# Expert weights split during the second mixture into the buffers that TensorE reads

## The chip, the cores and the metric

The kernel runs on one core of one Trainium2 chip. The metric is the device time of one execution in microseconds (us); lower is better. The kernel before took 1017.65 us, the median of three runs (1014.8 to 1020.23).

## What is computed

Three stages follow one another. Attention over 4 batches of 576 tokens gives x, 2304 tokens of width 512. A gated layer of width 1536 follows, then a mixture of 8 experts, of which each token takes the best two. In the reference, shortened:

```python
gate = 1 / (1 + exp(-(x @ w_gate)))          # first mixture: 2304 x 512 x 1536, twice
x = (gate * (x @ w_val)) @ w_out
noisy = x @ rg + log1p(exp(x @ rn)) * noise  # router, 8 experts
top2 = the two best experts of each token, weights = softmax of their two logits
for e in range(8):                           # second mixture
    h = relu(x[rows of e] @ w1[e])           # 512 x 1024
    out[rows of e] += weight * (h @ w2[e])   # 1024 x 512
```

## The kernel before, in words

Every fp32 operand of a large product is held as two fp16 halves, a high part and the rest, and a product is three fp16 matmuls (high by high, high by rest, rest by high). `split` (line 338) makes the halves of a tile: one activation on ScalarE writes the high part (line 339), one scalar_tensor_tensor on VectorE the rest (line 340). Ahead of a split stands a scale: the sum of squares of the whole matrix (two quarters by ScalarE, line 604, two by VectorE, line 602), added over the partitions by a small matmul with ones on TensorE and turned into a power of two by three short VectorE instructions (`norm2`, line 70).

The first mixture works through nine chunks of 256 tokens. `stage1` (line 373) makes gate times value of a chunk, `stage2` (line 402) multiplies by the output matrix, `tokens` (line 413) writes the 128 rows of a tile to DRAM as halves (`xs<-row`, line 429), turns them by a transposing DMA (`xt<-row`, line 432) and multiplies them by the router matrix (`pl`, line 439); `route` (line 492) picks the experts and scatters (token, weight) into a table in DRAM (line 554). The output matrix lies in the tiles `wob[0..5]`.

Beside the chunks runs `presplits` (line 577). For each of 16 units, the matrices w1 and w2 of 8 experts, it loads four quarters of 512 KB (`f<-w`, line 591; nine buffers), squares, scales and splits them into a tile `hl` (two buffers) and stores the halves to DRAM (`wsp<-hl`, line 619). One step is taken after each piece of a chunk; what is left ahead of the last chunk is taken in one go (`drain(pre)`, line 919).

The second mixture, `moe2` (line 719), goes expert by expert. `first2` (line 673) makes the hidden layer, eight tiles of 24 matmuls each, whose results ScalarE reads out (lines 684 and 685) and VectorE finishes (line 686, the low half of `hT`). `second2` (line 688) makes five tiles of 24 matmuls, which ScalarE scales (line 699) and GpSimd adds into the output by an indirect DMA (line 700). The rows of the next expert are fetched meanwhile: `fetch` (line 649) reads its part of the table on SP's queue, `gather` (line 663) collects rows by an indirect DMA of GpSimd, `turn` (line 670) turns them by a transposing DMA on SP's queue. w1 and w2 have two buffers each; `wload2` (line 645) loads the halves of expert e+2, 2 MB at a time, once expert e has left a buffer.

The instructions of each engine stand in an order that a scheduler makes from the program's order and from its own estimate of when each is ready; SP's queue too starts its DMAs in the order in which they stand, and one that waits holds up those behind it.

Of the kernel before, what the change touches and what calls it, by code (L numbers as in the profile page):

```python
# [9 lines left out]
F32 = mybir.dt.float32  # L10
# [30 lines left out]
SNAP = 6  # L41

# [14 lines left out]
class Kern:  # L57
# [284 lines left out]
    @staticmethod  # L342
    def flat(t):
        n = len(t.shape) - 1
        names = "abcd"[:n]
        return t if n == 1 else t.rearrange(f"p {' '.join(names)} -> p ({' '.join(names)})")
# [121 lines left out]
    def dram_open(self):  # L468
        dp = self.ctx.enter_context(self.tc.tile_pool(name="dram", bufs=1, space=DRAM))
        self.xs = dp.tile([N + PADS, 2 * DM], F16, name="xs")  # L470
        self.meta = dp.tile([P * NBLK, 2], I32, name="meta")
        self.wsp = dp.tile([E, P, 16384], F16, name="wsp")
# [99 lines left out]
    def presplit_open(self):  # L572
        self.ps_ctx = ExitStack()
        self.pp = self.ps_ctx.enter_context(self.tc.tile_pool(name="psp", bufs=2, side="right"))
        self.iv2 = self.cp.tile([P, 2, E], F32, name="iv2")

    def presplits(self):

        nc, a, pp = self.nc, self.a, self.pp
        units = [(e, j) for e in range(E) for j in range(2)]  # L580
# [44 lines left out]
    def inverse_scales(self):  # L625

        self.iw = self.cp.tile([P, E], F32, name="iw")
        self.nc.vector.scalar_tensor_tensor(self.iw, self.iv2[:, 0, :], 2.0 ** 19, self.iv2[:, 1, :], op0=ALU.mult, op1=ALU.mult)
# [89 lines left out]

    def moe2(self):

        mt, xe, xg = self.mt, self.xe, {}
        for e in range(E):
# [10 lines left out]
            if e + 2 < E:  # L733
                self.wload2(e + 2, 0)
# [10 lines left out]
            if e + 2 < E:  # L745
                self.wload2(e + 2, 1)

    def overflow(self):
# [23 lines left out]
        mt = cp.tile([P, 2], I32, name="mto")  # L772
        trips = nc.values_load(cnt[0:1, 0:1], min_val=0, max_val=E * EB)
        with self.tc.For_i(0, trips, 1):
# [18 lines left out]
            flat = lambda t: t.rearrange("p a b c -> p (a b c)")  # L793
            for j, w in enumerate((self.w1[0], self.w2[0])):
                nc.sync.dma_start(flat(w), self.wsp[ds(e, 1), :, j * 8192 : (j + 1) * 8192].rearrange("a p f -> p (a f)"))
# [7 lines left out]
    def build(self):  # L803
# [112 lines left out]
        for c in range(2, NCH):  # L916
            nxt = second_part(c - 1)
            if c == NCH - 1:
                drain(pre)
                self.ps_ctx.close()  # L920
                self.early_open()
                self.wload2(0, 0)
                self.inverse_scales()
                self.xe_tile(0)
# [65 lines left out]
```

## Time and profile before

| what | value |
|---|---|
| median of three runs | 1017.65 us |
| profiled execution, its own time | 1019.11 us |
| its span, first to last instruction | 1017.4 us |
| mean granted TensorE clock, share of full | 0.972 |
| TensorE matmuls busy | 962.5 us (95%) |
| VectorE busy | 469.4 us (46%) |
| ScalarE busy | 467.1 us (46%) |
| GpSimd busy | 214.3 us (21%) |
| DMA moved | 185.60 MB, mean 182 GB/s |

The attention fills about the first 185 us, the chunks of the first mixture 185 to 600 us, the second mixture the rest. A share over the whole span hides that the stages differ: VectorE and ScalarE do most of their work in the first 600 us. TensorE is the busiest engine by far, and the chain that ended last is a chain of TensorE over the whole second mixture.

### The profile page before, as it was taken

The page shows a single profiled execution, that of the slowest core. Times are in us where ns is not written, and L with a number is a line of the kernel's source. Part 1 is how long each engine was busy: PE and PEld are TensorE (multiplying, and loading weights), DVE is VectorE, ACT ScalarE, POOL GpSimd, SP SyncE. Part 2 cuts the span into 40 slices and gives each one's busy share as a digit, 9 for nine tenths or more (in the row PEclk, how much of TensorE's full clock was granted, in tenths as well). Part 3 has the DMA queues.
Part 4 walks back from the last instruction along what each step waited for, and adds up shares of the span by engine and source line. Part 5 has one row for each costly group of instructions (what it writes and reads, how often), then busy time and mean ns, then how long its engine had stood idle before and what let it go on. Part 6 is the DMA issues. An engine that isn't in the chain of part 4 may idle for free. (4 is left out here: it accounts for less than half of the span.)

```text
span 1017.4 us, 18817 instructions
## 1 busy us (share of the span) xinstructions
PE 962.5 (95%) x7471; PEld 674.8 (66%) x7471; DVE 469.4 (46%) x1296; ACT 467.1 (46%) x971; POOL 214.3 (21%) x213
## 2 busy tenths in 40 slices
PE   6889899999999999899989988999999999999996
PEld 5666777778678877687767555656565666666663
DVE  2688998756666767575776250111111111111020
ACT  4667777645565656455654142332323232323231
POOL 1243455001010101010101124312212222222202
PEclk9898998999999999999989999999999999999998
DMA  8666675876657776657665848955758575755303
GB/s 258 216 216 237 218 214 193 332 208 183 192 188 218 233 227 212 205 165 216 187 208 202 264 136 149 224 186 126 195 124 197 123 197 123 197 123 115 41 11 41
DMA packets 137097, 185.60 MB, mean 182 GB/s; under 512 B 72752, under 2 KB 82096, under 8 KB 134960
## 3 DMA queue, kind: packets, MB, share of 16 engines
q1 hardware_dynamic: 127024, 163.64, 52.5%
q0 software_dynamic: 9984, 20.75, 11.3%
q8 instruction: 59, 0.97, 0.4%
q14 instruction: 30, 0.25, 0.1%
HBM read 113.13 MB, written 56.02 MB: 166 GB/s over the span
## 5 line engine op out<-in xcount | busy, mean ns | idle before, releaser
L389 PE MATMUL pg<-x,w 128*128 128x256 f16 (+3 forms) x3456 | 311.6, 251 | 1.6 <-DVE sg L396 0.9
L389 PEld LDWEIGHTS <-w 128*128 128x128 f16 x3456 | 273.8, 100 | 33.9 <-issue 2.6
L694 PEld LDWEIGHTS <-hT 128*128 128x128 f16 (+1 forms) x960 | 100.1, 104 | 105.9
L411 PE MATMUL px<-wo,gT 128*128 128x512 f16 x648 | 147.2, 379 | 0.0
L686 DVE TENSOR_TENSOR hT<-r,hT 128x312 f16<-128x312 f32 (+2 forms) x128 | 56.9, 481 | 149.7 <-ACT hT L685 149.7
L554 POOL DMA_INDIRECT meta<-mt,vi x36 | 37.9, 1054 | 353.5 <-DVE sg L396 196.7
L680 PE MATMUL ph<-xe,w1a 128*128 128x312 f16 (+2 forms) x768 | 104.6, 299 | 3.4 <-DMA xe<-xg 3.4
L699 ACT ACTIVATE y<-py,css 128x512 f32<-128x512 f32 (+1 forms) x40 | 27.5, 687 | 174.9 <-PE py L694 170.4
L411 PEld LDWEIGHTS <-gT 128*128 128x128 f16 x648 | 62.4, 98 | 66.6
L700 POOL DMA_INDIRECT out<-y,mts x40 | 62.5, 1562 | 200.4 <-ACT y L699 198.9
L694 PE MATMUL py<-w2a,hT 128*128 128x512 f16 (+1 forms) x480 | 104.4, 379 | 0.0
L694 PE MATMUL py<-w2b,hT 128*128 128x512 f16 (+1 forms) x480 | 104.3, 379 | 0.0
L680 PE MATMUL ph<-xe,w1b 128*128 128x312 f16 x768 | 102.4, 296 | 0.0
L684 ACT ACTIVATE r<-ph 128x312 f32<-128x312 f32 (+2 forms) x128 | 48.9, 428 | 114.2 <-PE ph L680 111.5
L340 DVE SCALAR_TENSOR_TENSOR hl<-f,scs,hl 128x1024 f16<-128x1024 f32 x64 | 81.4, 1283 | 40.3 <-ACT hl L339 39.9
L339 ACT ACTIVATE hl<-f,scs 128x1024 f16<-128x1024 f32 x64 | 72.8, 1144 | 56.7 <-DMA wsp<-hl 40.6
L680 PEld LDWEIGHTS <-w1a 128*128 128x128 f16 x768 | 75.7, 99 | 31.3 <-DMA xe<-xg 3.9
L680 PEld LDWEIGHTS <-w1b 128*128 128x128 f16 x768 | 75.1, 98 | 27.1
L697 DVE TENSOR_TENSOR css<-mts,iw 128x1 f32<-128x1 f32 (+1 forms) x40 | 6.3, 159 | 183.5 <-ACT y L699 178.1
L395 ACT ACTIVATE sg<-pg,gs 128x256 f32<-128x256 f32 (+3 forms) x144 | 55.4, 410 | 20.5 <-PE pg L389 20.2
L398 ACT ACTIVATE gT<-sg 128x256 f16<-128x256 f32 x108 | 44.1, 410 | 44.4 <-DVE sg L396 44.4
L665 POOL DMA_INDIRECT xg<-xs,mts x40 | 40.1, 1003 | 114.3 <-issue 45.8
(300 smaller groups left out, 948.4 us busy)
## 6 DMA issues: line engine op xcount, KB each, us to landing
f<-w SPq DMA_DIRECT2D x64, 512.0 KB, 5.8
wsp<-hl SPq DMA_DIRECT2D x64, 512.0 KB, 3.9
w1a<-wsp SPq DMA_DIRECT2D x4, 2048.0 KB, 7.7
w2a<-wsp SPq DMA_DIRECT2D x4, 2048.0 KB, 8.7
w1b<-wsp SPq DMA_DIRECT2D x4, 2048.0 KB, 8.0
w2b<-wsp SPq DMA_DIRECT2D x4, 2048.0 KB, 7.8
w<-wg SPq DMA_DIRECT2D x12, 512.0 KB, 5.7
w<-wv SPq DMA_DIRECT2D x12, 512.0 KB, 5.7
```

The lines of the kernel that those rows point to most:

```text
L339: self.nc.scalar.activation(hi, src, AF.Copy, scale=sc)
L340: self.nc.vector.scalar_tensor_tensor(lo, src, sc, hi, op0=ALU.mult, op1=ALU.subtract)
L389: nc.tensor.matmul(pg[:, j, s:e], w[:, l, k, fo : fo + P], self.xT[b][r][:, k, t0 : t0 + e - s], start=n == 0, stop=n == 3 * KT - 1)
L395: nc.scalar.activation(sg[:, s:e], pg[:, 0, s:e], AF.Tanh, scale=self.gate_scale(b, u))
L398: nc.scalar.activation(g[:, 0, :], sg, AF.Copy, scale=2.0 ** -16)
L411: nc.tensor.matmul(p, g[:, l, t * P : (t + 1) * P], self.wob[f // 2][:, r, f % 2, :], start=f + i == 0, stop=f == FT - 1 and i == 2)
L665: self.nc.gpsimd.indirect_dma_start(out=xg.rearrange("p a b -> p (a b)"), out_offset=None, in_=self.xs[:rows, :], in_offset=bass.IndirectO ...
L680: nc.tensor.matmul(p[:, : t1 - t0], w1[:, l, k, f * P : (f + 1) * P], xe[:, x, t0:t1], start=n == 0, stop=n == 3 * KT - 1)
L684: nc.scalar.activation(r, p[:, : t1 - t0], AF.Relu, scale=2.0 ** -19)
L686: nc.vector.tensor_sub(self.hT[:, 1, f, t0:t1], r, self.hT[:, 0, f, t0:t1])
L694: nc.tensor.matmul(py, self.hT[:, l, f, i * P : i * P + m], w2[:, w, f, :], start=n == 0, stop=n == 3 * F2T - 1)
L700: d = nc.gpsimd.indirect_dma_start(out=self.out, out_offset=bass.IndirectOffsetOnAxis(ap=mt[:m, 0:1], axis=0), in_=y[:m], in_offset=None, ...
```

## The change

Only experts 0 and 1 are split ahead and go through DRAM (`AHEAD2 = 2`). The weights of experts 2 to 7 are loaded as fp32 during the second mixture, quarter by quarter, into the seven tiles `wob`, which the first mixture has left. There they are squared and split, straight into the w1 or w2 buffer that TensorE will read; the squares themselves go into the high half of that buffer, as a place to throw them. A generator (`splits`) does nine steps for each of the 12 units; two steps are taken after the first layer of an expert and three after each tile of its second layer. A quarter's buffer is loaded again once its split is done. A loop for experts with too many rows (`overflow`), whose weights came from DRAM too, now splits them anew as well; that part of the diff is left out.

```diff
+AHEAD2 = 2
...
-        self.wsp = dp.tile([E, P, 16384], F16, name="wsp")
+        self.wsp = dp.tile([AHEAD2, P, 16384], F16, name="wsp")
...
-        units = [(e, j) for e in range(E) for j in range(2)]
+        units = [(e, j) for e in range(AHEAD2) for j in range(2)]
...
-    def inverse_scales(self):
-
-        self.iw = self.cp.tile([P, E], F32, name="iw")
-        self.nc.vector.scalar_tensor_tensor(self.iw, self.iv2[:, 0, :], 2.0 ** 19, self.iv2[:, 1, :], op0=ALU.mult, op1=ALU.mult)
+    def inverse_scale(self, e):
+
+        self.nc.vector.scalar_tensor_tensor(self.iw[:, e : e + 1], self.iv2[:, 0, e : e + 1], 2.0 ** 19, self.iv2[:, 1, e : e + 1], op0=ALU.mult, op1=ALU.mult)
...
+    def part_load(self, j, i, e):
+
+        t = self.flat(self.wob[self.nparts % len(self.wob)]).bitcast(F32)
+        self.nparts += 1
+        self.nc.sync.dma_start(t.rearrange("p (k f) -> p k f", k=(KT, F2T)[j] // 4), self.part_src(j, i, e))
+        return t
+
+    def halves(self, j, i, x):
+
+        k = (KT, F2T)[j] // 4
+        return [self.flat((self.w1, self.w2)[j][x][:, l, i * k : (i + 1) * k, :]) for l in range(2)]
+
+    def splits(self):
+
+        nc = self.nc
+        units = [(e, j) for e in range(AHEAD2, E) for j in range(2)]
+        quarters = [(j, i, e) for e, j in units for i in range(4)]
+        parts = []
+
+        def load(n):
+            while len(parts) < min(n, len(quarters)):
+                parts.append(self.part_load(*quarters[len(parts)]))
+        load(len(self.wob))
+        for n, (e, j) in enumerate(units):
+            while self.freed[j] < e - 1:
+                yield
+            sums = self.my.tile([P, 4], F32, tag="sq", name="sq")
+            for i in range(4):
+                t, junk = parts[4 * n + i], self.halves(j, i, e % 2)[0].bitcast(BF16)
+                if i % 2:
+                    nc.vector.scalar_tensor_tensor(junk, t, 1.0, t, op0=ALU.mult, op1=ALU.mult, accum_out=sums[:, i : i + 1])
+                else:
+                    nc.scalar.activation(junk, t, AF.Square, accum_out=sums[:, i : i + 1])
+                yield
+            m = self.my.tile([P, 1], F32, tag="sm1", name="sm1")
+            nc.vector.tensor_reduce(m, sums, axis=AX.X, op=ALU.add)
+            s, iv = yield from self.norm2(self.my, m, "sc2")
+            nc.vector.tensor_copy(self.iv2[:, j, e : e + 1], iv)
+            if j:
+                self.inverse_scale(e)
+            for i in range(4):
+                self.split(parts[4 * n + i], s, *self.halves(j, i, e % 2))
+                load(len(self.wob) + 4 * n + i + 1)
+                yield
...
+    def step2(self, n):
+        for _ in range(n):
+            next(self.splitter, None)
...
+        self.freed, self.nparts = [0, 0], 0
+        self.splitter = self.splits()
...
             for f in range(F2T):
                 self.first2(self.w1[e % 2], xe[e], f, spans)
-            if e + 2 < E:
-                self.wload2(e + 2, 0)
+            self.step2(2)
+            self.freed[0] = e + 1
...
-            if e + 2 < E:
-                self.wload2(e + 2, 1)
+                self.step2(3)
+            self.freed[1] = e + 1
...
-                self.inverse_scales()
+                for e in range(AHEAD2):
+                    self.inverse_scale(e)
```

In the built programs the order moves at these places.

**SP's queue in the first mixture**, around the rows of the tenth tile of 128 tokens (`hl` are halves to be stored, `f` the next quarters). Before:

```order
L591 DMA f<-w 128x2x512
L619 DMA wsp<-hl 128x2x1024
L591 DMA f<-w 128x2x512
L429 DMA xs<-row 128x1024
L432 DMA_TRANSPOSE xt<-row 128x8x128
L619 DMA wsp<-hl 128x2x1024
L591 DMA f<-w 128x2x512
L619 DMA wsp<-hl 128x2x1024
```

After:

```order
L431 DMA xs<-row 128x1024
L434 DMA_TRANSPOSE xt<-row 128x8x128
L431 DMA xs<-row 128x1024
L434 DMA_TRANSPOSE xt<-row 128x8x128
L431 DMA xs<-row 128x1024
L434 DMA_TRANSPOSE xt<-row 128x8x128
L431 DMA xs<-row 128x1024
```

The stores and loads between the writes and the transposes are gone.

**SP's queue in the second mixture**, at the fetch for expert 3 (`mts` is the table, `xe<-xg` the turned rows). Before:

```order
L647 DMA w1b<-wsp 128x8192
L647 DMA w2b<-wsp 128x8192
L653 DMA mts<-meta 128x10
L671 DMA_TRANSPOSE xe<-xg 128x8x128 x5
L647 DMA w1a<-wsp 128x8192
L647 DMA w2a<-wsp 128x8192
```

After (`wo` are the tiles `wob`, `w` the fp32 weights):

```order
L643 DMA wo_73<-w 128x1024
L643 DMA wo_74<-w 128x1024
L643 DMA wo_75<-w 128x1024
L707 DMA mts<-meta 128x10
L725 DMA_TRANSPOSE xe<-xg 128x8x128 x5
L643 DMA wo_76<-w 128x1024
L643 DMA wo_77<-w 128x2x512
L643 DMA wo_71<-w 128x2x512
```

The 2 MB loads are gone, and quarters stand ahead of and behind the five turns; `wo_76<-w` is the last quarter of w1 of expert 4.

**VectorE in the second mixture**, expert 2. Before, its first layer, its five tiles and the next first layer:

```order
L686 TENSOR_TENSOR hT<-r,hT 128x312 x16
L697 TENSOR_TENSOR css<-mts,iw 128x1 x2
L697 TENSOR_TENSOR css<-mts,iw 112x1
L697 TENSOR_TENSOR css<-mts,iw 128x1 x2
L686 TENSOR_TENSOR hT<-r,hT 128x312 x16
```

After, from the middle of its first layer (`w1a,sq` are squares of expert 4, written into the w1 buffer of expert 2):

```order
L740 TENSOR_TENSOR hT<-r,hT 128x312 x2
L342 SCALAR_TENSOR_TENSOR w2b<-wo_72,sc2s,w2b 128x1024
L740 TENSOR_TENSOR hT<-r,hT 128x312 x6
L669 SCALAR_TENSOR_TENSOR w1a,sq<-wo_74 128x1024
L669 SCALAR_TENSOR_TENSOR w1a,sq<-wo_76 128x1024
L674 TENSOR_REDUCE sm_9060<-sq 128x1
L740 TENSOR_TENSOR hT<-r,hT 128x312 x2
L751 TENSOR_TENSOR css<-mts,iw 128x1
L82 TENSOR_SCALAR sc2h<-pmx 128x1
L83 TENSOR_SCALAR sc2s<-sc2h 128x1
```

Two squares and their sum stand ahead of the last two instructions on `hT` of this first layer.

## Rows read from the trace of the kernel before

**Rows 1.** Windows: us; busy of PE, PEld, DVE, ACT, POOL; clock; DMA share; GB/s.
```profile
185.00:600.00 415.00, 399.37 (x3959) 301.13 (x3958) 263.48 (x769) 223.31 (x413) 36.16 (x45) 0.98 0.68 212
648.00:1008.00 360.00, 359.32 (x2185) 218.88 (x2182) 55.17 (x151) 105.39 (x260) 81.05 (x62) 1.00 0.58 133
```

**Rows 2.** The chain that ended last, in order of time: start us, us, what.
```profile
637.57 10.36 PE py L694 x48
...
699.27 25.44 PE ph L680 x192
```

**Rows 3.** Waits, 185 to 600 us: engine line, releaser: us in total, times, longest.
```profile
PE pl L439 <- DMA xt<-row: 10.6, 4, 4.3
```

**Rows 4.** TensorE in order of time: start us, us, line, what [idle before <-releaser].
```profile
276.88 0.46 PE L439 MATMUL pl<-wr,xt 128*128 128x16 f16 x12 [2.21 <-DMA xt<-row]
...
277.19 7.07 PE L389 MATMUL pg<-x,w 128*128 128x256 f16 x48
...
387.22 0.17 PE L536 MATMUL pk<-o,tri 128*128 128x8 f16 x1 [0.89 <-DVE o L531]
...
429.02 0.49 PE L439 MATMUL pl<-wr,xt 128*128 128x16 f16 x12 [4.31 <-DMA xt<-row]
...
429.37 8.09 PE L389 MATMUL pg<-x,w 128*128 128x192 f16 x96
...
464.60 5.40 PE L389 MATMUL pg<-x,w 128*128 128x256 f16 x48
...
482.27 0.46 PE L439 MATMUL pl<-wr,xt 128*128 128x16 f16 x12 [1.73 <-DMA xt<-row]
...
482.58 7.05 PE L389 MATMUL pg<-x,w 128*128 128x256 f16 x48
...
528.11 0.49 PE L439 MATMUL pl<-wr,xt 128*128 128x16 f16 x12 [4.08 <-DVE gT L399]
...
528.83 7.82 PE L389 MATMUL pg<-x,w 128*128 128x256 f16 x48
```

**Rows 5.** The same view of VectorE and of SP's queue, ahead of 429 and 528 us.
```profile
416.91 2.48 DVE L340 SCALAR_TENSOR_TENSOR hl<-f,scs,hl 128x1024 f16<-128x1024 f32 x2 [0.84 <-ACT hl L339]
...
421.99 1.82 SPq L432 DMA_TRANSPOSE xt<-row  x1
...
523.98 2.47 DVE L340 SCALAR_TENSOR_TENSOR hl<-f,scs,hl 128x1024 f16<-128x1024 f32 x2
```

**Rows 6.** Everything on tile f: duration ns min/median/max, first and last start us, forms.
```profile
L339 ACT ACTIVATE hl<-f,scs x64: 1132/1148/1154, 210.5 to 547.8; 128x1024 f16<-128x1024 f32 x64
L340 DVE SCALAR_TENSOR_TENSOR hl<-f,scs,hl x64: 1274/1284/1287, 211.7 to 549.3; 128x1024 f16<-128x1024 f32 x64
L604 ACT ACTIVATE junk<-f x32: 1039/1057/1059, 195.4 to 519.2; 128x1024 bf16<-128x1024 f32 x32
...
L602 DVE SCALAR_TENSOR_TENSOR junk<-f x32: 1204/1222/1291, 196.9 to 521.8; 128x1024 bf16<-128x1024 f32 x32
...
DMA to landing us min/median/max: 4.2/5.8/10.7
```

**Rows 7.** Lines of the second mixture: engine op xcount | busy us, mean ns | idle, releaser.
```profile
L686 DVE TENSOR_TENSOR hT<-r,hT 128x312 f16<-128x312 f32 x112 | 49.2, 481 | 135.8 <-ACT hT L685 135.8
```

**Rows 8.** SP's queue in order of time, second mixture, third expert.
```profile
708.00 0.33 SPq L653 DMA_DIRECT2D mts<-meta  x1
...
713.64 10.84 SPq L671 DMA_TRANSPOSE xe<-xg  x5
```

**Rows 9.** Landing of the scatter of y: four of the second expert, then the fifth.
```profile
DMA to landing us min/median/max: 4.8/4.8/4.9
...
DMA to landing us min/median/max: 7.6/7.6/7.6
```

**Rows 10.** GpSimd's scatter of the routing table: 200 to 600 us, then the whole span.
```profile
L554 POOL DMA_INDIRECT meta<-mt,vi x28 | 30.2, 1079 | 316.9 <-DVE sg L396 196.7 <-DVE vi L551 78.2 <-issue 42.0
...
L554 POOL DMA_INDIRECT meta<-mt,vi x36 | 37.9, 1054 | 353.5 <-DVE sg L396 196.7
```

More of the change, by code (lines that the diff above doesn't have):

```diff
@@ L575, in presplit_open @@
         self.iv2 = self.cp.tile([P, 2, E], F32, name="iv2")
+        self.iw = self.cp.tile([P, E], F32, name="iw")
     def presplits(self):
         nc, a, pp = self.nc, self.a, self.pp
-        units = [(e, j) for e in range(E) for j in range(2)]
+        units = [(e, j) for e in range(AHEAD2) for j in range(2)]
         parts, sums = [], {}
@@ L622, in presplits, with part_src @@
                 yield
-    def inverse_scales(self):
-        self.iw = self.cp.tile([P, E], F32, name="iw")
-        self.nc.vector.scalar_tensor_tensor(self.iw, self.iv2[:, 0, :], 2.0 ** 19, self.iv2[:, 1, :], op0=ALU.mult, op1=ALU.mult)
+    def inverse_scale(self, e):
+        self.nc.vector.scalar_tensor_tensor(self.iw[:, e : e + 1], self.iv2[:, 0, e : e + 1], 2.0 ** 19, self.iv2[:, 1, e : e + 1], op0=ALU.mult, op1=ALU.mult)
+    def part_src(self, j, i, e):
+        k = (KT, F2T)[j] // 4
+        w = self.a[("w1", "w2")[j]]
+        src = w[e].rearrange("(k p) f -> p k f", p=P) if isinstance(e, int) else w[e].rearrange("a (k p) f -> p (a k) f", p=P)
+        return src[:, i * k : (i + 1) * k]
@@ new lines, in part_load @@
+    def part_load(self, j, i, e):
[4 more added lines that the diff above has]
+    def halves(self, j, i, x):
+        k = (KT, F2T)[j] // 4
+        return [self.flat((self.w1, self.w2)[j][x][:, l, i * k : (i + 1) * k, :]) for l in range(2)]
[29 more added lines that the diff above has]
+                yield
@@ L772, in overflow @@
         mt = cp.tile([P, 2], I32, name="mto")
+        s2 = cp.tile([P, 4], F32, name="s2")
         trips = nc.values_load(cnt[0:1, 0:1], min_val=0, max_val=E * EB)
@@ L792, in overflow @@
             b = nc.sync.value_load(be[0:1, 1:2], min_val=0, max_val=E * EB - 1)
-            flat = lambda t: t.rearrange("p a b c -> p (a b c)")
-            for j, w in enumerate((self.w1[0], self.w2[0])):
-                nc.sync.dma_start(flat(w), self.wsp[ds(e, 1), :, j * 8192 : (j + 1) * 8192].rearrange("a p f -> p (a f)"))
+            for j in range(2):
+                nc.vector.tensor_tensor(mo, m, self.iv2[:, j, :], op=ALU.mult)
+                nc.vector.tensor_reduce(s2[:, j : j + 1], mo, axis=AX.X, op=ALU.add)
+                nc.vector.tensor_scalar(s2[:, 2 + j : 3 + j].bitcast(I32), s2[:, j : j + 1].bitcast(I32), -1, 254 << 23, op0=ALU.mult, op1=ALU.add)
+                for i in range(4):
+                    self.split(self.part_load(j, i, ds(e, 1)), s2[:, 2 + j : 3 + j], *self.halves(j, i, 0))
             nc.sync.dma_start(mt, self.meta.rearrange("(p c) t -> p c t", p=P)[:, ds(b, 1), :].rearrange("p c t -> p (c t)"))
```

## The prediction

> **What bounds the kernel now.** I read the windows first, to see which stage has room. From 185 to 600 us, the first mixture, TensorE is busy 399.4 of 415 us, VectorE 263 and ScalarE 223. From 648 to 1008 us, in the second mixture, TensorE is busy 359.3 of 360 us at a granted clock of 1.00, while ScalarE has 105 us of work and VectorE 55 [rows 1]. The chain of waits is TensorE alone there, 25.44 us for a first layer and 5.18 us for a tile of the second (10.36 for two) [rows 2]. So the second mixture can't get shorter by this change: whatever is gained must come out of the first mixture, and what is put into the second can only cost.
>
> Then the waits of TensorE, and TensorE in order of time, show what there is to gain. TensorE waits four times for the transposed rows `xt`, 10.6 us in all [rows 3]. Three of these, at 276.9, 429.0 and 482.3 us, lie beside the splits; the fourth (10.6 less 8.25, 2.4 us) comes at the end, past the last split. Two more waits are for VectorE: 0.89 us at 387.2 and 4.08 us at 528.1 us [rows 4]. A long wait costs more than itself: 48 matmuls of 256 columns take 5.40 us in an undisturbed place, but 7.07, 7.05 and 7.82 us right behind three of the waits, and the same columns in 96 pieces take 8.09 us behind the one at 429.0 [rows 4].
>
> **What the change removes.** 48 of 64 quarters are no longer loaded, squared, split and stored in the first mixture; its steps run out in the chunk that runs around 300 us. Why the splits stand behind the waits is seen at 429.0: VectorE does two splits (2.48 us from 416.9) ahead of the low half of the rows, the transpose is issued at 422.0, and it lands 7.0 us later [rows 4, 5], with quarters in SP's queue ahead of it (the order of that queue above). At 528.1 it is the same engine: two splits from 524.0, 2.47 us, ahead of what the router's matmul stands behind [rows 5]; this is where the remaining steps are taken at once. Without the splits the rows are ready about 2.5 us sooner and the queue holds nothing but rows. Each term is the wait and the excess behind it [rows 4]:
>
> - 387.2: 0.9
> - 429.0: 4.31 + (8.09 - 5.40) = 7.0
> - 482.3: 1.73 + (7.05 - 5.40) = 3.4
> - 528.1: 4.08 + (7.82 - 5.40) = 6.5
>
> That is 17.8 us. The wait at 276.9 is 2.21 + (7.07 - 5.40) = 3.9 us, but splits of expert 1 are still running there. No quarter is loaded beside them any more, only halves stored; one store still stands ahead of the transpose. Its bounds are 0 and 3.9; I take 3.0, nearer the top, since the wait is only 2.2 us and the loads go. The twelve small matmuls for the scales move from one stage to the other and cancel. The last wait for `xt`, the routing tail and the first gathers keep their order and their cost. The overflow loop isn't entered: no DMA of its line is among the trace's issues.
>
> **What it adds, and what hides it.** For each of six experts ScalarE gets 4 squares of 1.06 us and 8 splits of 1.15 us, 13.4 us, and VectorE 4 of 1.22 and 8 of 1.28, 15.1 us [rows 6]. Over the second mixture that makes ScalarE 105 + 80 = 185 and VectorE 55 + 91 = 146 of 360 us: both stay under half. The bytes loaded there are the same, 4 MB an expert, as fp32 in place of two halves. TensorE hides all this as long as no instruction in an in-order queue is late. Three places could be:
>
> (1) The first sum, for expert 2, stands on TensorE ahead of expert 1's first layer, at 637.57 + 10.36 = 647.9 us. Its buffer is free at 637.6 [rows 2], and its quarters are loaded as soon as the first mixture has left the tiles. Two squares on each engine need about 3 us, against 10. Nothing is lost.
>
> (2) The splits stand between read-outs of the first layer, up to three in a row, 3.4 us on ScalarE. TensorE needs 25.44 / 8 = 3.2 us for one of the eight tiles, and its buffers let it run a tile ahead. That is close, but it holds. I put 1.5 us for one or two short waits in the whole stage.
>
> (3) In experts 2 to 5 the last quarter of the next w1 stands in SP's queue behind the five turns, and its square stands on VectorE ahead of the last two instructions on `hT`, which the last matmuls of the first tile of the second layer need. Take expert 2, which starts at 699.3 us. The turns end at 713.64 + 10.84 = 724.5, that is 25.2 us in [rows 8]. A quarter lands 4.2 (the least) to 5.8 us (the median) later [rows 6]; the square and one instruction on `hT`, 1.2 + 0.2 + 0.5 us, follow [rows 6, 7]. TensorE needs it 22 matmuls into the tile, at 25.4 + 22 x 5.18 / 24 = 30.2 us in. With the turns where they are the result is there at 31.3 to 32.9, late by 1.1 to 2.7 us. But the turns themselves come sooner now: the fetch at 708.0 waits for the last scatter of y, which lands after 7.6 us while a 2 MB load runs beside it, and after 4.8 us where none does [rows 8, 9], and these loads are gone. 2.8 us sooner, the result is there at 28.5 to 30.1, just in time. I take zero here and keep the late case as a rival.
>
> **The sum.** Against the profiled execution's own 1019.1 us (span 1017.4): 1019.1 - 17.8 - 3.0 + 1.5 = 999.8 us. That execution lies 1.5 us above the median of the three runs, so against the median the forecast is **998.3 us**, 1.9% less. About 0.5% (5 us) is what a measurement of this kernel can tell from no change.
>
> **Rival 1, the late quarter.** If the turns don't move up, place (3) costs 1.1 to 2.7 us in each of four experts, and 1.7 us of slower matmuls behind each, as behind the shorter waits of rows 4: 11 to 18 us, so 1009 to 1016 us, about 1012. For it: the turns are a chain of gathers and transposes of its own. Against: rows 9. Chance 0.16, half of it within 0.5% of before.
>
> **Rival 2, slower: GpSimd held up by the splits.** Scatters and gathers of GpSimd read their row numbers from SBUF, and the split's VectorE instruction reads two operands there. If each of the last scatter and five gathers waited for a whole split, 1.28 us, the turns would end 6 x 1.28 = 7.7 us later than at 22.4 us in, the quarter's result would be there at 36.2 to 37.8, and TensorE would lose 6.0 to 7.6 us and some 2.4 us behind it, four times: about 36 us, 1034 us. It turns slower than before once an expert loses more than 19.3 / 4 = 4.8 us, a wait of about 3.1 us at place (3). The trace speaks against it: GpSimd's scatter takes 1.08 us among the splits; the other eight of the 36, with none beside them, take (37.9 - 30.2) / 8 = 0.96 us [rows 10], so 0.1 us each and not 1.28. Chance 0.09. The Trainium skill, page "SBUF — State Buffer", section "Who interferes with whom", states the rule by which this would happen: a VectorE instruction with two inputs in SBUF and a GpSimd instruction that reads SBUF exclude one another for the whole of the instruction; the 0.1 us of rows 10 agree only if few of them meet.
>
> **Rival 3, no gain.** The waits for `xt` could come from the transposes themselves and stay; then only the two waits for VectorE go, 7.4 us, and one or two short waits come: near 1012 to 1018 us. Against it stand the 7.0 us of rows 4 and 5, with quarters in the way. Chance 0.07.
>
> **How the numbers follow.** Forecast 0.68, rivals 0.16, 0.09 and 0.07. Faster by over 0.5% (below 1012.6): 0.68 + half of rival 1, 0.08, gives 0.76. Slower by over 0.5%: 0.09. The rest, 0.15, is the same. The forecast's own bounds are 996 us (all of the 3.9 us, nothing lost) and some 1004; single runs of the kernel lie up to 2.9 us below its median, so the low end is 993. Going up, the range takes in most of rival 1, to 1014.
>
> **What would show it.** In the profile after: no wait of TensorE for `xt` or VectorE between 300 and 560 us, and the first mixture some 18 to 21 us shorter. In the second, a first layer still 25.4 us and a tile 5.2 us; VectorE near 146 and ScalarE near 185 us of busy time there. A wait of TensorE for VectorE (the `hT` line) at the head of the second layers of experts 2 to 5 would be rival 1 or, if the turns end past 25 us in and GpSimd's instructions grow by a microsecond, rival 2. Waits for `xt` that stay would be rival 3. The prediction is wrong if the first mixture shortens by less than 14 us, or the second grows by more than 6.

## The result, and the profile after

The change took the time from 1016.22 us (four runs, 1013.71 to 1020.23) to **1001.42 us** (four runs, 999.31 to 1002.47): ratio 0.985, 95% interval 0.981 to 0.989. The forecast was 998.3 us, the range 993 to 1014.

One thing told above has to be put right: the two steps of `splits` stand inside the loop over the tiles of the first layer, so two are taken after each of its eight tiles, not two after the layer (the diff above shows that line indented too little). The prediction was worked out from the built order, so no number of it hangs on this.

Lines stand two to 54 lower in the changed kernel: `pl` is L441, the splits L341 and L342, the squares L669 and L671, the first layer L734, `hT` L740, the second layer L748.

The page of the kernel after, busy time of each engine and what the DMA moved (185.60 MB before):

```profile
PE 954.1 (96%) x7471; PEld 668.6 (67%) x7471; DVE 481.3 (48%) x1303; ACT 470.3 (47%) x971; POOL 217.9 (22%) x213
...
DMA packets 122313, 135.27 MB, mean 135 GB/s; under 512 B 71792, under 2 KB 81136, under 8 KB 121712
```

VectorE and ScalarE have as much work as before; it lies elsewhere. The windows of the kernel after, in answer to [rows 1] (the second is 24 us earlier, at the same place of the program):

```profile
185.00:600.00 415.00, 411.53 (x4064) 305.60 (x4061) 188.89 (x657) 160.59 (x332) 47.81 (x59) 1.00 0.37 104
624.00:984.00 360.00, 357.22 (x2189) 218.51 (x2188) 145.24 (x301) 174.71 (x347) 84.39 (x60) 1.00 0.60 124
```

In the first mixture TensorE has 3.5 us of idle time in 415, where it had 15.6, and the DMA moves 104 GB/s, where it moved 212. In the second it has 2.8 us of idle time, where it had 0.7.

The waits of the kernel after, 185 to 600 us, in answer to [rows 3]:

```profile
ACT hl L341 <- DMA wsp<-hl: 4.7, 5, 2.0
DVE junk L605 <- DMA f<-w: 2.0, 2, 1.3
PE pl L441 <- DMA xt<-row: 1.8, 1, 1.8
ACT junk L607 <- DMA f<-w: 1.3, 1, 1.3
PE pk L538 <- DVE o L533: 0.5, 1, 0.5
```

The same view of the kernel before, two lines on ScalarE that the prediction did not use:

```profile
ACT hl L339 <- DMA wsp<-hl: 40.6, 25, 2.8
ACT junk L604 <- DMA f<-w: 28.9, 13, 5.6
```

ScalarE stood 40.6 us ahead of splits, until one of the two buffers for halves had been stored, and 28.9 us ahead of squares, until a quarter had landed.

TensorE of the kernel after in order of time, in answer to [rows 4]: every wait for an engine or a DMA of over 0.2 us from 200 us on.

```profile
565.69 0.74 PE L441 MATMUL pl<-wr,xt 128*128 128x16 f16 x23 [1.76 <-DMA xt<-row]
579.68 0.17 PE L538 MATMUL pk<-o,tri 128*128 128x8 f16 x1 [0.46 <-DVE o L533]
602.10 11.68 PE L734 MATMUL ph<-xe,w1a 128*128 128x240 f16 x96 [3.34 <-DMA xe<-xg]
706.46 5.79 PE L748 MATMUL py<-w2a,hT 128*128 128x512 f16 x26 [0.22 <-DVE hT L740]
811.01 5.79 PE L748 MATMUL py<-w2a,hT 128*128 128x512 f16 x26 [1.15 <-DVE hT L740]
864.21 5.79 PE L748 MATMUL py<-w2b,hT 128*128 128x512 f16 x26 [1.41 <-DVE hT L740]
```

The five waits between 270 and 530 us are gone. The rest of expert 0's first layer, at 625.90 us before, starts at 602.10. Until there, attention took 1.6 us more in this execution, so the first mixture is 25.4 us shorter. From there to the end of the last second layer it is 386.4 us, against 381.4: 5.0 us more (the expectations below say 4.8). With 0.1 us of tail that makes the 18.7 us between the spans (1017.4 and 998.7).

What the prediction adds as the excess behind a wait is a lower granted clock. Windows of the kernel before, behind the wait at 429.0 and at the undisturbed place, then one of the kernel after, behind one of its new waits (the clock is the third number from the end):

```profile
429.40:437.50 8.10, 8.10 (x103) 7.87 (x100) 3.81 (x17) 4.43 (x9) 0.00 (x0) 0.67 0.44 173
464.60:470.00 5.40, 5.40 (x50) 4.79 (x49) 4.72 (x12) 3.24 (x6) 0.00 (x0) 1.00 0.68 178
811.00:817.00 6.00, 5.99 (x30) 2.90 (x31) 0.56 (x3) 0.85 (x2) 1.62 (x1) 1.00 0.55 120
```

Of TensorE's two levels, 2.4 and 1.2 GHz, the first of these stretches has both (0.50 from 429.4 to 434 us), behind a wait of 4.31 us; the other two, the last behind a wait of 1.15 us, are at the full clock throughout.

Three new waits, 2.78 us in all, stand 22 matmuls into the second layer of experts 2, 4 and 5: place (3). (Two expectations below speak of the first layer there; the second is meant.) SP's queue of the kernel after in order of time, the five turns that run beside each of experts 2 to 5, in answer to [rows 8]:

```profile
687.43 12.83 SPq L725 DMA_TRANSPOSE xe<-xg  x5
739.72 11.12 SPq L725 DMA_TRANSPOSE xe<-xg  x5
791.21 13.45 SPq L725 DMA_TRANSPOSE xe<-xg  x5
845.55 12.40 SPq L725 DMA_TRANSPOSE xe<-xg  x5
```

The first layers of these experts start at 675.75, 727.76, 779.37 and 832.31 us, so the turns end 24.5, 23.1, 25.3 and 25.6 us in; the waits are 0.22, none, 1.15 and 1.41 us. VectorE of expert 5, the same view:

```profile
862.27 1.22 DVE L669 SCALAR_TENSOR_TENSOR w1b<-wo 128x1024 bf16<-128x1024 f32 x1 [4.36 <-DMA wo<-w]
...
863.68 0.87 DVE L740 TENSOR_TENSOR hT<-r,hT 128x312 f16<-128x312 f32 x2
```

The square waits for the last quarter, which SP issues behind the turns (they end at 857.95 us), and the last two instructions on `hT` wait behind the square. The turns do start sooner, 11.7 us into expert 2, where they started 14.4 us in before, but this is partly undone by their lasting longer: 11.1 to 13.5 us, where they took 10.1 to 11.2. One difference is seen on VectorE and GpSimd, in order of time, at the turns of expert 2:

```profile
686.67 1.12 POOL L719 DMA_INDIRECT xg<-xs,mts  x1 [0.30 <-issue]
...
687.88 2.48 DVE L342 SCALAR_TENSOR_TENSOR w2b<-wo,sc2s,w2b 128x1024 f16<-128x1024 f32 x2 [0.52 <-ACT w2b L341]
...
688.09 1.90 POOL L719 DMA_INDIRECT xg<-xs,mts  x1 [0.30 <-issue]
```

The gather that starts inside a split takes 1.90 us, its neighbour 1.12: it ends 0.83 us after the first split (1.28 of the 2.48 us) does. It is so with one or two of the five gathers of every expert from 2 to 6; they take 1.18 to 1.94 us, some 0.82 us more than what is left of the split, and the others 0.94 to 1.13. But this gather, the fourth, is not what sets the end of the turns. The fifth gather starts when the first turn has landed, and the last turn when the fifth gather has. At expert 2 the first turn landed after 6.9 us, where it took 5.2 before, and the fifth gather after 4.0 us (3.6 before): that is the 2.0 us. At experts 4 and 5 the first turn landed after 5.6 and 6.0 us (3.9 to 5.2 before), and the fifth gather of expert 4 after 5.9 (3.6 to 4.3 before). Why they landed later is not shown. Over all, lines of the second mixture, 600 us to the end, after (the first line answers to [rows 7]) and before:

```profile
L740 DVE TENSOR_TENSOR hT<-r,hT 128x312 f16<-128x312 f32 (+1 forms) x120 | 52.3, 475 | 80.9 <-ACT hT L739 80.4
...
L719 POOL DMA_INDIRECT xg<-xs,mts x33 | 38.2, 1157 | 65.8 <-DMA xe<-xg 30.3 <-DMA mts<-meta 24.1 <-issue 11.4
```

```profile
L665 POOL DMA_INDIRECT xg<-xs,mts x37 | 37.2, 1006 | 98.2 <-issue 45.2 <-DMA xe<-xg 44.8 <-DMA mts<-meta 8.2
```

### The profile page after: what moved, and what is told of

Same layout as the page of the kernel before. It is cut to its first block, busy times and chain, and to the rows that moved or that the text cites. A ratio compares the mean times of both kernels' runs of the same rounds, so it can differ in the third digit from the quotient of the medians.

```text
span 998.7 us, 18707 instructions
## 1 busy us (share of the span) xinstructions
PE 954.1 (96%) x7471; PEld 668.6 (67%) x7471; DVE 481.3 (48%) x1303; ACT 470.3 (47%) x971; POOL 217.9 (22%) x213
## 4 chain that ended last, share of the span: by engine, by line
PE 78%; DVE 8%; DMA 7%; ACT 2%; issue 2%; POOL 1%; SPq 0%; POOLq 0%; DVEq 0%; ACTq 0%
PE pg L391 26%; PE py L748 18%; PE ph L734 16%; PE px L413 13%; DMA xe<-xg 2%; DMA xg<-xs,mts 1%; PE pa L159 1%; DMA wo<-w 1%; PE pa L217 1%; DVE w L342 1%; DVE w L292 1%; DVE gT L401 1%; DMA phi<-phi 1%; DVE wo L292 1%; PE pa L168 1%
## 5 line engine op out<-in xcount | busy, mean ns | idle before, releaser
L391 PE MATMUL pg<-x,w 128*128 128x256 f16 (+3 forms) x3456 | 303.9, 248 | 0.8 <-ACT th L239 0.6
L391 PEld LDWEIGHTS <-w 128*128 128x128 f16 x3456 | 268.4, 99 | 31.3 <-issue 2.4
L748 PEld LDWEIGHTS <-hT 128*128 128x128 f16 (+1 forms) x960 | 99.9, 105 | 108.2 <-DVE hT L740 4.3
L734 PE MATMUL ph<-xe,w1a 128*128 128x312 f16 (+2 forms) x768 | 105.0, 299 | 3.3 <-DMA xe<-xg 3.3
L748 PE MATMUL py<-w2a,hT 128*128 128x512 f16 (+1 forms) x480 | 105.0, 379 | 1.4 <-DVE hT L740 1.4
L748 PE MATMUL py<-w2b,hT 128*128 128x512 f16 (+1 forms) x480 | 104.8, 379 | 1.4 <-DVE hT L740 1.4
L734 PE MATMUL ph<-xe,w1b 128*128 128x312 f16 x768 | 102.9, 296 | 0.0
L740 DVE TENSOR_TENSOR hT<-r,hT 128x312 f16<-128x312 f32 (+2 forms) x128 | 56.8, 480 | 83.0 <-ACT hT L739 82.5
L734 PEld LDWEIGHTS <-w1a 128*128 128x128 f16 x768 | 75.8, 99 | 31.0 <-DMA xe<-xg 3.8
L398 DVE SCALAR_TENSOR_TENSOR sg<-sg,pg 128x256 f32<-128x256 f32 x108 | 45.1, 418 | 104.7 <-ACT sg L397 104.0
L734 PEld LDWEIGHTS <-w1b 128*128 128x128 f16 x768 | 75.2, 98 | 26.8
L401 DVE SCALAR_TENSOR_TENSOR gT<-sg,gT 128x256 f16<-128x256 f32 x108 | 52.4, 486 | 31.9 <-ACT gT L400 31.7
L719 POOL DMA_INDIRECT xg<-xs,mts x40 | 44.9, 1124 | 75.3 <-DMA xe<-xg 30.3
L739 ACT CAST hT<-r 128x312 f16<-128x312 f32 (+2 forms) x128 | 52.5, 461 | 0.4
```

The costliest lines, as they stand in the source:

```text
L391: nc.tensor.matmul(pg[:, j, s:e], w[:, l, k, fo : fo + P], self.xT[b][r][:, k, t0 : t0 + e - s], start=n == 0, stop=n == 3 * KT - 1)
L398: nc.vector.scalar_tensor_tensor(sg, sg, 1.0, pg[:, 1, :], op0=ALU.add, op1=ALU.mult)
L401: nc.vector.scalar_tensor_tensor(g[:, 1, :], sg, 2.0 ** -16, g[:, 0, :], op0=ALU.mult, op1=ALU.subtract)
L719: self.nc.gpsimd.indirect_dma_start(out=xg.rearrange("p a b -> p (a b)"), out_offset=None, in_=self.xs[:rows, :], in_offset=bass.IndirectO ...
L734: nc.tensor.matmul(p[:, : t1 - t0], w1[:, l, k, f * P : (f + 1) * P], xe[:, x, t0:t1], start=n == 0, stop=n == 3 * KT - 1)
L739: nc.scalar.copy(self.hT[:, 0, f, t0:t1], r)
```

## Experiments

Every kernel below was compared with the kernel before on the same chip. Where a run puts work of experts 2 to 7 back beside the first mixture, its second mixture is still the changed kernel's.

**1. Put it all back beside the first mixture.**

```diff
...
-        units = [(e, j) for e in range(AHEAD2) for j in range(2)]
+        units = [(e, j) for e in range(E) for j in range(2)]
```

> The changed kernel, with the splits of experts 2 to 7 put back beside the first mixture as extra work: loads, squares, splits and stores as before, for halves that nothing reads; the second mixture splits them again as in the changed kernel. Theory (all of the gain comes from these splits standing beside the first mixture): the five waits of TensorE come back, the first mixture is as long as before the change, and the whole is the kernel before plus what the second mixture lost, 4.8 us: about 1021 us. Rival (the gain comes from something else that the change moved, as the 2 MB loads or the last steps taken at once with the drain): 1001 to 1008 us.

1021.26 us, ratio to before 1.003 (1.001 to 1.006). The gain is gone, so all of it came from the first mixture. The waits there, same view as above:

```profile
ACT hl L341 <- DMA wsp<-hl: 40.6, 25, 3.0
ACT junk L607 <- DMA f<-w: 28.4, 16, 5.0
PE pl L441 <- DMA xt<-row: 13.9, 6, 4.4
...
PE pk L538 <- DVE o L533: 2.3, 1, 2.3
```

TensorE waits six times for rows here, four times before. One of the two more is the wait at 528.1, which the profile before puts down to VectorE:

```profile
526.69 0.49 PE L441 MATMUL pl<-wr,xt 128*128 128x16 f16 x12 [4.36 <-DMA xt<-row]
```

In the kernel before both came within 0.03 us of one another: the transpose issued at 524.51 landed 3.6 us later, and `gT` was done at 528.09. So the wait at 528.1 was one for rows as well, and only the 0.89 us at 387.2 were VectorE's alone.

**2. The engines' work alone.** Squares, sums and splits as in run 1, with quarters that are already on chip; no load and no store for experts 2 to 7.

```diff
...
             e, j = units[n]
+            if e >= AHEAD2:
+                parts.append(parts[-8])
+                return
...
-                nc.sync.dma_start(dst[:, :, i * 1024 : (i + 1) * 1024], hl)
+                if e < AHEAD2:
+                    nc.sync.dma_start(dst[:, :, i * 1024 : (i + 1) * 1024], hl)
```

> As the run before, but for experts 2 to 7 only the work of the engines is put back beside the first mixture (squares, the small sums, splits, on quarters that lie there already): no load and no store for them. The halves so made are read by nobody. Theory A (the waits come from VectorE and ScalarE being taken when the rows need them): the waits for VectorE at 387 and 528 come back, 7.4 us, with 1.7 us of small matmuls, and part of those for the turned rows: 1010 to 1016 us. Theory B (they come from the transfers, ahead of the rows in SP's queue and beside them): 1002 to 1006 us.

1003.2 us, ratio 0.984 (0.981 to 0.988): within 2 us of the changed kernel, 1.7 of them the twelve small matmuls, which this run does in both stages. Its window shows VectorE and ScalarE as busy as before, and TensorE too:

```profile
185.00:600.00 415.00, 412.09 (x4072) 306.21 (x4070) 266.86 (x807) 232.98 (x428) 50.24 (x58) 1.00 0.35 102
```

So the time that the splits take of VectorE and ScalarE is not what cost.

**3. The transfers alone.** 48 loads, and 48 stores of the loaded quarters to a scratch area; no square and no split.

```diff
...
+                for i in range(4):
+                    nc.sync.dma_start(dst[:, :, i * 512 : (i + 1) * 512], parts[4 * n + i].rearrange("p (t f) -> p t f", t=2))
+                    load()
+                    yield
+                continue
```

> The other half: for experts 2 to 7 only the transfers are put back beside the first mixture, 48 loads of 512 KB and 48 stores of 512 KB from the same tiles to a place in DRAM that nothing reads, with no square, sum or split. Theory A: the waits for VectorE stay away and those for the turned rows come back in small part: 1001 to 1005 us. Theory B: the three waits for the turned rows come back, 2 to 7 us each with what follows them: 1010 to 1016 us. If both are needed for a wait to form (rows 2.5 us late, and a transpose of 7 us in place of 3 to 5), each of the two runs gives back less than its share, and their sum is less than that of the run with all.

1017.78 us, ratio 1.000 (0.997 to 1.003). The waits come back without the splits. But here a load waits until the store that empties its buffer has ended, where before the split freed the buffer; SP's own waits in this kernel:

```profile
SPq L595 <- DMA scr<-f: 72.3, 35, 5.7
```

Writes of rows stood up to 10.4 us in SP's queue after the row was done, so the run says that transfers can do it, and not by which way. The kernel before was profiled once more:

> The kernel before, unchanged, for a second profile: its single times spread over 6.5 us, and the prediction's terms come from one execution near the top of them. If the waits of TensorE in the first mixture vary, this profile has others, of another total than 17.8 us between 300 and 560 us, at the same places in the order; if they are fixed by the order alone, the same five waits to a few tenths.

1017.17 us. The waits are at the same places and at one more (0.88 us at 458.7), of other sizes: 3.72 us where it had been 0.89, at 386.4 us, and 0.93 where it had been 4.31, at 427.5. The wait at the place of 528.1 is put down to rows here too.

**4 and 5. Loads without stores, stores without loads.** Both with the engines' work.

> The changed kernel with the engines' work of experts 2 to 7 (squares, sums, splits) and their 48 loads of 512 KB put back beside the first mixture, but not their 48 stores; the second mixture is the changed kernel's, so the output is the reference's. Two of the three things that were there before; the engines' work alone gave 1003.2 us, all three 1021.3 us. If what held the first mixture is the stores, because in SP's queue the writes of the rows stand behind stores that wait for their splits: 1003 to 1006 us, rows written within 1 us of being done, landings of the rows' transposes 4 to 5 us. If it is the mere traffic beside the transposes: about half of the 18 us come back, 1010 to 1014 us, with landings of 5 to 7 us and again waits for the rows in the first mixture. If the loads are what holds ScalarE and VectorE (splits that wait for a load, ahead of a row in the order of the engine): rows done late, 1010 us or more with landings unchanged.

> The changed kernel with the engines' work of experts 2 to 7 and their 48 stores of 512 KB put back, but not their 48 loads: what is split there again and again are quarters of expert 1 that are already on chip, and nothing reads what is stored for experts 2 to 7; the second mixture is the changed kernel's, so the output is the reference's. If it is the stores in SP's queue ahead of the rows' writes (held 4 to 8 us in the kernel before): 1014 to 1020 us, with rows' writes issued 3 us and more after the row is done at three or four tiles. If it is the traffic: 1010 to 1014 us, by longer landings with the issue at once. If it is the loads: 1003 to 1006 us.

1008.92 us with the loads (ratio 0.993, 0.990 to 0.996) and 1007.32 us with the stores (0.990, 0.986 to 0.993). Against run 2 that is 5.7 and 4.1 us by the medians; both together are 18.1. The first two lines are of the waits with the loads, the fence behind it with the stores:

```profile
ACT junk L607 <- DMA f<-w: 38.2, 21, 4.0
ACT hl L341 <- DMA wsp<-hl: 9.0, 6, 2.5
```

```profile
ACT hl L341 <- DMA wsp<-hl: 14.0, 15, 2.5
```

None of the theories had it: neither side alone carries the cost. That both together cost more than the two added is likely and not certain: by the ratios they add up to 0.014 of 0.019, a difference within the intervals. With both, ScalarE's wait for a buffer goes from 9.0 and 14.0 us to 40.6.

**6. Stores on GpSimd's queue.**

```diff
-                nc.sync.dma_start(dst[:, :, i * 1024 : (i + 1) * 1024], hl)
+                (nc.sync if e < AHEAD2 else nc.gpsimd).dma_start(dst[:, :, i * 1024 : (i + 1) * 1024], hl)
```

> All of the work on experts 2 to 7 beside the first mixture again (that alone gave 1021.3 us), but their 48 stores are issued by GpSimd, on a queue of its own, instead of by SP ahead of the rows' writes. The second mixture is the changed kernel's, the output the reference's. If SP's queue is the cause: the rows are written within 1 us of being done, and 1003 to 1008 us. If it is the traffic, or engines that wait for the two buffers of split quarters to be stored: 1014 to 1021 us, with waits for rows again. More than 1021 us would say that GpSimd's own queue is the worse place.

1074.48 us, ratio 1.054 (1.050 to 1.058): GpSimd's queue is much the worse place. The waits, 185 to 600 us:

```profile
POOL wsp L622 <- DVE hl L342: 152.3, 34, 15.5
ACT hl L341 <- DMA wsp<-hl: 57.4, 22, 7.1
...
PE pk L538 <- DVE o L533: 21.9, 3, 11.9
```

A store issued late keeps its buffer, ScalarE waits for the buffer up to 7.1 us, and the routing on VectorE stands behind the split that ScalarE is late with. It does not separate the theories, as SP's queue was not the only thing changed.

**7. Four buffers for halves**, paid for with seven instead of nine for loaded quarters; all else as in run 1.

```diff
...
-FB = 9
+FB = 7
...
-                hl = pp.tile([P, 2048], F16, tag="hl", name="hl").rearrange("p (t f) -> p t f", t=2)
+                hl = pp.tile([P, 2048], F16, tag="hl", bufs=4, name="hl").rearrange("p (t f) -> p t f", t=2)
```

> All of the work on experts 2 to 7 beside the first mixture again (that alone gave 1021.3 us), with four buffers instead of two for the split quarters that wait for their store, paid for with seven instead of nine buffers for loaded quarters. The second mixture is the changed kernel's, the output the reference's. If ScalarE and VectorE stand in order behind splits that wait for a store to end (40.6 us of such waits on ScalarE before), and the rows with them: these waits fall under 10 us, 1008 to 1014 us. If it is the landing of the transposes beside the traffic, or SP's queue: 1018 to 1024 us.

1012.0 us, ratio 0.993 (0.990 to 0.995), where run 1 had 1.003. With the same bytes and the same work, about half of the 18 us is gone. The waits of ScalarE and TensorE, 185 to 600 us:

```profile
ACT junk L607 <- DMA f<-w: 32.2, 19, 4.4
...
PE pk L538 <- DVE o L533: 4.1, 2, 2.9
PE pl L441 <- DMA xt<-row: 2.4, 4, 1.3
```

There is no line for `hl` and its store any more, and TensorE's 13.9 us for rows are 2.4. SP's queue is free too: the writes of the rows go out within 0.2 us of the row. How it was held in the kernel before is seen at the eleventh tile of rows; VectorE, ScalarE and SP in order of time:

```profile
446.10 0.75 DVE L428 SCALAR_TENSOR_TENSOR row<-px,tts,row 128x512 f16<-128x512 f32 x1 [0.23 <-ACT row L427]
...
450.56 1.15 ACT L339 ACTIVATE hl<-f,scs 128x1024 f16<-128x1024 f32 x1 [1.97 <-DMA wsp<-hl]
...
453.05 0.38 SPq L619 DMA_DIRECT2D wsp<-hl  x1
...
454.70 0.62 SPq L429 DMA_DIRECT2D xs<-row  x1
```

The row is done at 446.85. Ahead of its write SP has a store whose split ScalarE can't start until an earlier store has ended; the write goes out 7.85 us late. In run 7 the same write goes out 0.03 us after its row. TensorE did not wait for this very tile in that execution. Of the four tiles whose rows it did wait for between 270 and 530 us, two lay done for 3.9 and 4.7 us until SP wrote them (276.9 and 482.3), and two were written within 0.3 us of being done (429.0 and 528.1): there the rows themselves were late. Ahead of the row of 528.1 two splits on ScalarE had waited 1.90 and 2.75 us for a buffer (513.24 and 517.81). At 429.0 ScalarE of the kernel before shows why:

```profile
411.48 1.06 ACT L604 ACTIVATE junk<-f 128x1024 bf16<-128x1024 f32 x1 [5.63 <-DMA f<-w]
```

A square waits for its load, and the gate of the next chunk on ScalarE, then VectorE and the row stand behind it. In run 7 that square waits 2.45 us, and TensorE 0.47 for the row.

**8. The same, each store and load one step later in SP's queue**, behind a row's write made in between.

```diff
...
                 self.split(parts[4 * n + i], s, hl[:, 0, :], hl[:, 1, :])
-                nc.sync.dma_start(dst[:, :, i * 1024 : (i + 1) * 1024], hl)
-                load()
                 squares(n + 1, i)
-                yield
+                if 4 * n + i < 4 * len(units) - 1:
+                    yield
+                nc.sync.dma_start(dst[:, :, i * 1024 : (i + 1) * 1024], hl)
+                load()
+                if 4 * n + i == 4 * len(units) - 1:
+                    yield
```

> As the run with four buffers for split quarters, but each store and load is put into SP's queue one step of the presplits later, so that its splits are done when SP comes to it and a row's write made in between goes ahead of it. The second mixture is the changed kernel's, the output the reference's. If SP's queue, in which rows stood 4 to 8 us behind stores, carries a part of the cost: 4 us or more less than the run with four buffers, every row written within 1 us of being done. If only the traffic is left: no difference to that run, landings of the rows' transposes still 5 us and more.

1010.07 us, ratio 0.993 (0.990 to 0.995), the same as run 7: with four buffers SP's order carries nothing more that can be told from noise. With two, it was not tried by itself. The landings of the rows' transposes settle nothing, as only two of 18 are on record here (3.1 and 5.5 us; medians of 4.4 in the changed kernel and 5.8 in run 1). But the same traffic costs half as much with four buffers, so a mere crowd of transfers is not the cause of that half.

The profiles give the first mixture by itself, free of the rest of an execution: us from TensorE's last matmul of the attention to the start of the rest of expert 0's first layer.

| kernel | first mixture, us |
|---|---|
| before, two profiles | 450.25, 448.77 |
| after, two profiles (the second is run 9's) | 424.85, 424.44 |
| 1, all put back | 449.82 |
| 2, engines' work alone | 428.28 |
| 4, with the loads | 437.27 |
| 5, with the stores | 432.21 |
| 7, all, four buffers | 437.19 |
| 8, the same, stores and loads later | 436.22 |

Each is one execution, and equal code differs by up to 3 us (424.77 and 427.42 in the two profiles with the eighth buffer). Over run 2 the loads cost 9.0 us, the stores 3.9, both 21.5; four buffers take away 12.6. What is left, 8 to 9 us, is what the loads cost alone and goes with ScalarE's 30 us of waits for them. That the loads are the whole of the rest was not tried.

**9. An eighth buffer for quarters in the second mixture**, for the new waits. With eight, all quarters of an expert stand ahead of the fetch and the turns.

```diff
...
-        t = self.flat(self.wob[self.nparts % len(self.wob)]).bitcast(F32)
+        t = self.flat(self.ring[self.nparts % len(self.ring)]).bitcast(F32)
...
-        load(len(self.wob))
+        load(len(self.ring))
...
-                load(len(self.wob) + 4 * n + i + 1)
+                load(len(self.ring) + 4 * n + i + 1)
...
+        self.ring = self.wob + [mb.tile([P, 2, 2, DM], F16, name=f"wx{i}") for i in range(1)]
```

> The changed kernel with an eighth buffer for quarters in the second mixture (from the pool of the outputs' tiles), so that all eight quarters of an expert can be asked for ahead of the splits that free the next one. The three waits of TensorE in the second mixture (0.22, 1.15 and 1.41 us, all at the 22nd matmul of an expert's first layer, the first on the last quarter of the weights) go if their cause is that the last quarter's load waits for a buffer: 998.6 us, ratio to the changed kernel 0.997. If their cause is the splits on VectorE and ScalarE themselves, or the load's own landing: 1001 to 1002 us, the waits stay. Buffers handed round in another order can shift which quarter is late: up to 1004 us.

994.95 us, ratio to before 0.977 (0.974 to 0.979). Behind the first group of expert 0, no wait is left in the second mixture. VectorE in order of time, at the first layer of expert 4:

```profile
802.14 1.22 DVE L669 SCALAR_TENSOR_TENSOR w1a<-wo 128x1024 bf16<-128x1024 f32 x1
...
803.28 1.22 DVE L669 SCALAR_TENSOR_TENSOR w1a<-wo 128x1024 bf16<-128x1024 f32 x1
...
804.76 0.88 DVE L741 TENSOR_TENSOR hT<-r,hT 128x312 f16<-128x312 f32 x2
```

Both squares follow without a wait, though the five turns end 24.5 us into the layer, as late as at the changed kernel's first wait. This run and the changed kernel had stood beside before on different chips, so both were run again on one:

> The changed kernel unchanged, on the same chip as the run with the eighth buffer, to set the two side by side: 1000 to 1003 us, the waits of the second mixture again at the 22nd matmul of an expert's first layer and of about 1 us each, TensorE's first group of expert 0 again at the lower clock behind its wait of some 3 us. If the waits or that wait are chance, they are elsewhere or of another size here.

> The changed kernel with the eighth buffer for quarters once more, beside the changed kernel on one chip. The first run gave 995.0 us; its second mixture was 4.8 us shorter than the changed kernel's, 2.8 of them the three waits and 1.7 a first group of expert 0 that ran at the full clock, behind a shorter wait. If the second of these was chance: 3 to 5 us less than the changed kernel. If it belongs to the edit: 6 to 7 us less, and the first group at the full clock again.

996.96 us (996.32 to 1004.56) and 994.55 us (992.68 to 996.03), ratios to before 0.980 (0.978 to 0.983) and 0.976 (0.975 to 0.978). The extra buffer is worth 2.4 us by the medians, close to the 2.8 us of waits, and 4.2 by the ratios, give or take some 3. The first group of expert 0 takes 10.01 us in both here, so the 11.68 us of the first profile do not come from the seven buffers. The changed kernel's waits, 2.5 us in all, stood in part elsewhere; VectorE and TensorE, second mixture:

```profile
632.53 1.23 DVE L669 SCALAR_TENSOR_TENSOR w2a<-wo 128x1024 bf16<-128x1024 f32 x1 [4.65 <-DMA wo<-w]
...
634.74 3.60 PE L734 MATMUL ph<-xe,w1b 128*128 128x312 f16 x24 [1.53 <-ACT r L738]
...
808.69 5.79 PE L748 MATMUL py<-w2a,hT 128*128 128x512 f16 x26 [0.76 <-DVE hT L740]
```

The mechanism is the same at both: a square waits on VectorE for a quarter (4.65 us, and 3.70 at 806.75), and `hT` behind it. Of all kernels run, this one with eight buffers is the fastest.

## Why the prediction was right, and where it was off

**What bounds the kernel**: right. The whole gain came out of the first mixture (run 1), and the second only lost. That the total came out so near is in part luck: in the profiles the first mixture gave 4.6 us more than forecast and the second took 3.5 us more.

**What the change removes**: the places were right, all five waits went. Forecast were 17.8 + 3.0 = 20.8 us, measured 25.4. The wait at 276.9 went whole, 3.9 us and not 3.0 (0.9 more); the twelve small matmuls left this stage (12 x 0.14 = 1.7 us), which the prediction said would cancel, as they do only over both stages; the last wait for rows fell from 2.38 to 1.76 us. Some 1.4 us are not traced.

**The cause** was half wrong. The step that failed is "Without the splits the rows are ready about 2.5 us sooner", with VectorE's two splits ahead of the rows as the reason at 429.0 and 528.1. Run 2 puts all the splits back and keeps the gain. At 528.1 the two splits even stand behind the row (523.31, the splits 523.98), and the wait read as VectorE's was one for rows (run 1). What holds the rows is the waiting of ScalarE ahead of splits and squares: ahead of splits for one of two buffers whose store has not ended (four buffers give back half or more, run 7), and ahead of squares for loads (the rest has their size, run 4). A row or a routing step that stands behind such an instruction waits with it, and SP's queue, where the prediction had put the rest, is held by the same splits; which of the two ways carried how much was not separated. The sum came out because it was taken from TensorE's waits, whatever stood behind these. Its terms one by one are chance: the waits at 387.2 and 429.0 were 3.72 and 0.93 us in the second profile of before, and the four waits of the sum 11.0 and 10.6 us in all.

**What it adds**: VectorE 145 us of 360 (forecast 146), ScalarE 175 (185); a first layer stays at 25.4 us, a tile at 5.2. Place (1) cost nothing, as forecast; place (2), for which 1.5 us were put, cost nothing in the first profile and 1.53 us in the repeat, there by a late quarter and not by splits in a row. Place (3) was the mis-sized term: taken as zero, it cost 0.22, 1.15 and 1.41 us. The step that failed is "2.8 us sooner", for the end of the turns: the last scatter of y landed after 4.49 us, as [rows 9] had it, and the turns started 2.7 us sooner, but they got slower and ended 23.1 to 25.6 us in, not 22.4. In sum the second mixture grew by 5.0 us: 2.78 of waits and 1.7 of small matmuls, with 0.5 us not traced, against 1.5 forecast and 1.7 said to cancel.

**Rival 1** had this mechanism and its size for one expert (1.1 to 2.7 us late with the turns at 25.2 us in). Its price was too high: the matmuls behind these short waits are not slowed. 26 of them take 5.79 us in all three rows, 5.77 behind no wait (814.45 us of the repeat), and the clock stays at 1.00. **Rival 2** had a mechanism that is real and a price that was not. A gather inside a split loses 0.2 to 1.0 us by itself (1.18 to 1.94 against 0.94), less than the whole split that was feared, and one or two gathers of an expert meet one, not all six instructions, so the mean grew by 0.15 us. The 0.1 us that spoke against it [rows 10] was such a mean, too. At expert 2 the gather that met a split did not set the end of the turns; landings did. The Trainium skill, page "SBUF — State Buffer", section "Who interferes with whom", states that a VectorE instruction with two inputs in SBUF and a GpSimd instruction that reads SBUF exclude one another for the whole instruction; these rows agree as to the gather, which waits for the rest of the split, and show no split held up by a gather: the two of 2.48 us, the second of which starts inside it, take no longer than two elsewhere [rows 5]. **Rival 3** fell with the waits.

## What to carry to other kernels

Work that hides beside a bottleneck is not priced by its busy time: VectorE, with a third of its time free, and ScalarE, with nearly half, still delayed what stood behind an instruction that waited for a buffer or a load. So look at what the covering engines wait for, not only at the waits of the engine that bounds: two more buffers for halves, at the price of two for quarters, gave back half or more of what moving all the traffic away did. And where loads share a queue with a chain of other DMAs, give them the buffer that lets the whole batch stand ahead of that chain.

## What the runs showed that was not expected

- Loads alone cost 5.7 us and stores alone 4.1, both together 18.1 by the medians (9.0, 3.9 and 21.5 by the profiles): the two sides seem to cost more together than added, which the intervals do not make certain.
- Beside experts 2 to 6, a gather that starts inside a split takes 0.82 us and what is left of the split, to 0.01 us at seven of seven (0.36 to 1.12 us were left). One more, which starts within 0.01 us of a split's own start, takes 0.95 us.
- The same 512 KB stores issued from GpSimd made the kernel 5.4% slower than before; GpSimd stood 152.3 us ahead of them.
- The very same changed kernel gave medians of 1001.42 and 996.96 us beside 1016.22 and 1018.85 of before in two sittings; a comparison of two variants across sittings is good to some 4 us only.
